# Windowed attention and a gated feed-forward on one core: a planner's order gives way to a table of 1334 numbers

## The chip, the cores and the metric

The kernel runs on 1 core of one Trainium2 chip. The metric is device time in microseconds (us) of one execution; less is better.

## The reference

Four batches of 768 tokens. Attention has 8 heads of 64; each chunk of 32 queries sees 8 memory keys and its own context of 56 keys (16 to the left, 8 to the right, fewer at the ends). Its output goes through a feed-forward network whose hidden layer is gated by a convolution over three tokens.

```python
for c in range(nc):                       # 24 chunks of 32 queries
    k_full = concat([mem_k, k[l_start:r_end]])
    scores = scale * q_c @ k_full.T
    a = exp(scores - max(scores))
    a = a / (sum(a) + 1e-9)
    out[c] = a @ v_full
x = out as (B, S, 512)
h = maximum(x @ w_in, 0.0)                # 512 -> 1024
conv_out = sum over k of conv_w[k] * h shifted by k - 1 tokens
return (h * sigmoid(conv_out)) @ w_out    # 1024 -> 512
```

All inputs but the weights are float32; the weights w_in, conv_w and w_out come as 64-bit floats and are turned into pairs of float32 numbers (hi and lo) on the chip.

## The kernel before, in words

Attention works in 32 steps, eight a batch: a step is one half of the tokens (hf) and two heads. The first four steps are groups of their own, the others go two by two, which makes 18 groups. A group loads q, k and v (L473), computes scores on the tensor engine (PE) into the psum tile s (L485), takes the maximum on the vector engine (DVE, L402), subtracts it (L408) and takes exp on the scalar engine (ACT, L414), or does both on ACT (L433). Sums (L451), 1e-9 (L455), reciprocal (L458) and the product that normalizes (L461) follow; 1e-9 and the product run on DVE or on GpSimd (POOL), by the strings ZADD and NORM. PE transposes the probabilities into tile t (L509), ACT copies them to w_t (L516), PE multiplies by v (L524), and ACT and DVE split the result into x_hi (L537) and x_lo (L540).

The feed-forward has eight blocks (fc) of 128 hidden features. For each block and half, PE adds up four times three products of x and w_in in one of four psum banks f (L563: hi by hi, hi by lo, lo by hi), and ACT takes the relu (L580). When both halves of a block are there, the convolution runs over all 768 tokens: the first tap on ACT (L590) or DVE (L594) by TAP, two more on DVE (L600); ACT takes the sigmoid (L604); the product with h is on DVE or POOL (L608) by MULT; ACT rounds to hi (L618) and DVE or POOL subtracts to get lo (L621) by LO. Then PE adds up eight times three products with w_out for each of six tiles of tokens, in a bank f again (L639), ACT copies it out (L651) and SP stores it (L654).

Sixteen blocks of weights, 512 KB each, are loaded (L285) into a ring of four tiles w64 and converted by from_f64: ACT takes the absolute value (L288), DVE shifts and masks (L292 to L339), POOL adds or multiplies (L334 to L357). W_IN and W_OUT name one of several ways for each.

What sets the order: every call of plan.op records an operation with its engine, a cost in ns, a due time, the tiles that it reads and writes. Plan.run then plays the whole program by these costs: an engine that is free takes, of the operations that could start at once, the one with the least due time (with a penalty for a change of the activation table or of PE's mode). The due times are linear in the step or block, with constants in DUE. Operations are emitted in the order in which this play started them, and each engine and queue works in the order of emission. All loads and stores are issued by SP into one queue. A tile comes from a ring with a fixed number of buffers: f has 4, w64 4, s and t one each; a new tile can be made only when the last use of the one that many places before has been emitted.

```python
            t, e, i = best
            ...
            do()
            self.times.append((t, end, e, i))
```

Of the kernel before, what the change touches and what calls it, by code (L numbers as in the profile page):

```python
# [2 lines left out]

# [5 lines left out]

# [6 lines left out]

CH, LEFT, RIGHT, NMEM = 32, 16, 8, 8  # L20
# [35 lines left out]
class Tile:


    def __init__(self, ring, make):
        self.ring, self.make, self.t, self.left, self.due = ring, make, None, 0, None  # L60


class Plan:

    def __init__(self):
        self.ops, self.last, self.readers = [], {}, defaultdict(list)
        self.rings, self.parts = {}, defaultdict(list)  # L70
# [4 lines left out]
    def op(self, eng, cost, due, do, r=(), w=(), shared=False, table=None, mode=None, late=70):  # L75

# [18 lines left out]
        tiles = dict.fromkeys(x[0] if isinstance(x, tuple) else x for x in (*r, *w))  # L95
        tiles = [x for x in tiles if isinstance(x, Tile)]
        for x in tiles:
            x.left += 1
# [4 lines left out]
    def over(self, k):

        if not isinstance(k, tuple):
            return [k, *self.parts[k]]
# [4 lines left out]
    def run(self):
        ops = self.ops
        n = len(ops)
        users = [[] for _ in range(n)]
        need = [0] * n
        for i, o in enumerate(ops):
            need[i] = len(o[4])
            for a in o[4]:
                users[a].append(i)
        ready = [0.0] * n  # L120
        cand = defaultdict(list)
        for i in range(n):
            if not need[i]:
                cand[ops[i][0]].append(i)
        free, shared_free, queue_free = defaultdict(float), 0.0, 950.0
        table = mode = None
        last_use = {}

        queue = defaultdict(list)
        for x in dict.fromkeys(x for o in ops for x in o[5]):  # L130
            queue[x.ring].append(x)
        for c in queue.values():
            c.sort(key=lambda x: x.due)
        self.times = []
        for _ in range(n):
            best = None
            for e, c in cand.items():
                at = []
                for i in c:
                    t = max(ready[i], free[e])  # L140
                    if ops[i][6]:
                        t = max(t, shared_free) if e == "V" else t
                    ok = True
                    for x in ops[i][5]:
                        if x.t is None:
                            size, used = self.rings[x.ring]
                            if queue[x.ring][len(used)] is not x:
                                ok = False
                                break
                            if len(used) >= size:  # L150
                                old = used[-size]
                                if old.left:
                                    ok = False
                                    break
                                t = max(t, last_use[old] + 70)
                    if ok:
                        at.append((t, i))
                if not at:
                    continue
                t0 = min(at)[0]  # L160
                i = min(
                    (ops[i][2] + (SWITCH if ops[i][7] and ops[i][7] != table else 0) + (MODE if ops[i][8] and ops[i][8] != mode else 0), i)
                    for t, i in at
                    if t <= t0 + 1
                )[1]
                if best is None or t0 < best[0]:
                    best = (t0, e, i)
            if best is None:
                raise RuntimeError("nothing can go on", [(i, *ops[i][:3], [x.ring for x in ops[i][5]]) for e in cand for i in cand[e] if e not in ('DMA','PE')][:12], dict((k, (len(v[1]), v[1][-v[0]].left if len(v[1])>=v[0] else 0, queue[k][len(v[1])].due if len(v[1])<len(queue[k]) else None)) for k, v in self.rings.items()))
            t, e, i = best  # L170
            eng, cost, due, do, after, tiles, shared, tab, md, late = ops[i]
            if tab and tab != table:
                cost += 1283
                table = tab
            if md and md != mode:
                cost += 95 if mode == "whole" else 140
                mode = md
            if e == "DMA":
                queue_free = max(queue_free, t + 600) + cost
                end, free[e] = queue_free + 1400, t + 60  # L180
            else:
                if shared:
                    t = max(t, shared_free)
                    shared_free = t + (cost * 0.78 if e == "G" else cost - 120)
                end = free[e] = t + cost
            cand[e].remove(i)
# [7 lines left out]
            self.times.append((t, end, e, i))
            for u in users[i]:
                ready[u] = max(ready[u], end + (late if ops[u][0] != e or e == "DMA" else 0))
                need[u] -= 1
                if not need[u]:
                    cand[ops[u][0]].append(u)
        return max(x[1] for x in self.times)  # L200


def vec(n, rate=1, ptr=0):
    return (140 + n / rate) / 0.96 + 62 * ptr


def act(n, psum=False, ptr=0):
    return ((192 if psum else 238) + n) / 1.2 + 93 * ptr

QB, KB, WB = 3, 2, 1

S_NS, A_NS = 520, 690
SWITCH, MODE = 78.9, 14.8


@with_exitstack  # L220
def attention_then_gated_ffn(
    ctx: ExitStack,
    tc: tile.TileContext,
    q: bass.AP,
    k: bass.AP,
    v: bass.AP,
    w_in: bass.AP,
    conv_w: bass.AP,
    w_out: bass.AP,
    out: bass.AP,  # L230
):
# [32 lines left out]

    def lin(name, i):
        return DUE[name][0] + DUE[name][1] * i

    def from_f64(src, hi, lo, key, n, kind, due, first):  # L270
# [535 lines left out]
```

## Time and profile before

| what | value |
|---|---|
| median of 3 runs | 359.49 us (358.17 to 363.31) |
| profiled execution, first to last instruction | 359.9 us |
| PE busy | 334.7 us |
| DVE, ACT, POOL busy | 244.8, 205.1, 126.4 us |
| mean granted clock of PE | 0.995 |
| read from memory, written | 35.55 MB, 6.29 MB |

The profile is of one execution. Its span runs from the first instruction to the last and is 0.4 us above the median of the runs, so little lies around it. Matmuls are pipelined: their records overlap, and a busy PE need not be at its peak. L485, L524 and L509 are float32; the trace has two matmuls and two weight loads where the program has one of L485 or L524.

### The profile page before, as it was taken

The numbers are of one execution on the slowest core, as the hardware profiler recorded it, in microseconds if no ns is written. First come the engines' busy times: TensorE is split into PE (matmuls) and PEld (weight loads), VectorE is DVE, ScalarE is ACT, GpSimd is POOL, SyncE is SP. The second block draws the span as 40 slices with busy tenths as digits, with TensorE's granted clock in tenths as the row PEclk, the third lists the DMA queues.
The fourth block names the chain that finished last, engine by engine and source line by source line (L and its number), as shares of the span: only waits on it lengthen the run. The fifth ranks groups of instructions, "written<-read, shape, count | busy, mean of one in ns | idle before, by whom it ended". The sixth has DMA issues, their size and how long they took to land.

```text
span 359.9 us, 10406 instructions
## 1 busy us (share of the span) xinstructions
PE 334.7 (93%) x4536; PEld 298.1 (83%) x4536; DVE 244.8 (68%) x319; ACT 205.1 (57%) x380; POOL 126.4 (35%) x154
## 2 busy tenths in 40 slices
PE   1497999996999999989999999999999999999996
PEld 0386999996999998778787889998887799998886
DVE  4877889997799899999993404889512228986100
ACT  3433666872978687779652417768453245584201
POOL 1566127922556636201656001252220001546000
PEclk9999999998999999999999999999999999999999
DMA  7978887777361153261202520000422000000111
GB/s 273 370 236 267 298 272 223 232 214 238 118 190 37 58 190 103 89 188 63 89 29 89 195 82 2 1 2 1 153 105 77 29 31 2 0 0 3 58 58 58
DMA packets 19917, 42.50 MB, mean 118 GB/s; under 512 B 2336, under 2 KB 10784, under 8 KB 19872
## 3 DMA queue, kind: packets, MB, share of 16 engines
q1 hardware_dynamic: 19872, 41.85, 35.1%
q8 instruction: 35, 0.57, 0.7%
q14 instruction: 10, 0.08, 0.1%
HBM read 35.55 MB, written 6.29 MB: 116 GB/s over the span
## 4 chain that ended last, share of the span: by engine, by line
PE 77%; DVE 13%; issue 4%; DMA 3%; ACT 2%; SPq 1%; POOL 0%; ACTq 0%; DVEq 0%
PE f L563 35%; PE f L639 27%; PE t L524 7%; PE s L485 4%; DVE c L600 4%; PE t L509 3%; DMA h<-in_k_dram 2%; DVE g L621 2%; DMA w<-in_w_out_dram 1%; DVE z L451 1%; SPq L473 1%; DVE x_lo L540 1%; DVE c L594 1%; DVE top L402 1%; DVE c L608 1%
## 5 line engine op out<-in xcount | busy, mean ns | idle before, releaser
L639 PE MATMUL f<-w_out_hi,g 128*128 128x512 f32 (+1 forms) x400 | 124.6, 388 | 0.1
L563 PE MATMUL f<-x_hi,w_in_hi 128*128 128x384 f32 x256 | 89.5, 349 | 0.0
L639 PEld LDWEIGHTS f<-w_out_hi,g 128*128 128x128 f32 x400 | 74.0, 188 | 16.5 <-DVE g L621 0.6
L563 PE MATMUL f<-x_hi,w_in_lo 128*128 128x384 f32 x256 | 86.9, 340 | 0.0
L563 PE MATMUL f<-x_lo,w_in_hi 128*128 128x384 f32 x256 | 86.8, 339 | 0.0
L639 PE MATMUL f<-w_out_lo,g 128*128 128x512 f32 (+1 forms) x200 | 77.1, 386 | 0.8 <-issue 0.8
L600 DVE SCALAR_TENSOR_TENSOR c<-h,cw,c 128x768 f32<-128x768 f32 x48 | 61.9, 1298 | 23.5 <-ACT c L590 22.1
L563 PEld LDWEIGHTS f<-x_hi,w_in_hi 128*128 128x128 f32 x256 | 48.6, 190 | 1.3 <-issue 0.5
L563 PEld LDWEIGHTS f<-x_hi,w_in_lo 128*128 128x128 f32 x256 | 48.8, 190 | 0.2
L563 PEld LDWEIGHTS f<-x_lo,w_in_hi 128*128 128x128 f32 x256 | 48.7, 190 | 0.0
L639 PEld LDWEIGHTS f<-w_out_lo,g 128*128 128x128 f32 x200 | 37.6, 188 | 8.8 <-issue 1.3
L608 POOL TENSOR_TENSOR c<-c,h 128x768 f32<-128x768 f32 x9 | 16.5, 1837 | 77.5 <-ACT c L604 75.4
L651 ACT COPY o_sb<-f 128x512 f32<-128x512 f32 (+1 forms) x25 | 14.2, 570 | 43.7 <-PE f L639 31.6
L580 ACT ACTIVATE h<-f 128x384 f32<-128x384 f32 x48 | 23.4, 491 | 21.6 <-PE f L563 21.1
L621 POOL TENSOR_TENSOR g<-c,g 128x768 fp32r<-128x768 f32 x12 | 25.7, 2144 | 22.0 <-ACT g L618 22.0
L604 ACT ACTIVATE c<-c 128x768 f32<-128x768 f32 x32 | 27.1, 846 | 10.4 <-DVE c L600 10.2
L524 PEld LDWEIGHTS t<-w_t,v_t 64*64 64x64 f32 x1536 | 25.4, 140 | 7.9 <-issue 4.3
L540 DVE TENSOR_TENSOR x_lo<-t,x_hi 128x768 fp32r<-128x768 f32 (+1 forms) x18 | 15.5, 862 | 23.5 <-ACT x_hi L537 23.4
L524 PE MATMUL t<-w_t,v_t 64*64 64x32 f32 x1536 | 27.5, 225 | 2.6 <-issue 1.3
L618 ACT CAST g<-c 128x768 fp32r<-128x768 f32 x24 | 20.0, 835 | 9.1 <-POOL c L608 6.4
L485 PE MATMUL s<-k_t,q_d 64*32 64x64 f32 x1344 | 18.6, 231 | 5.2 <-issue 4.7
L516 ACT COPY w_t<-t 128x768 f32<-128x768 f32 (+1 forms) x18 | 13.2, 732 | 17.4 <-PE t L509 17.4
(75 smaller groups left out, 439.0 us busy)
## 6 DMA issues: line engine op xcount, KB each, us to landing
v_t<-in_v_dram SPq DMA_DIRECT2D x32, 384.0 KB, 4.5
k_t<-in_k_dram SPq DMA_DIRECT2D x28, 252.0 KB, 4.1
out_dram<-o_sb SPq DMA_DIRECT2D x23, 256.0 KB, 2.0
q_d<-in_q_dram SPq DMA_DIRECT2D x28, 192.0 KB, 4.7
w<-in_w_in_dram SPq DMA_DIRECT2D x8, 512.0 KB, 5.2
w<-in_w_out_dram SPq DMA_DIRECT2D x8, 512.0 KB, 4.0
h<-in_k_dram SPq DMA_DIRECT2D x4, 252.0 KB, 7.0
h<-in_q_dram SPq DMA_DIRECT2D x4, 192.0 KB, 6.8
```

The source lines that it names most:

```text
L485: nc.tensor.matmul(s.t[w * CH : (w + 1) * CH, h ^ (w & 1), (i * NG + g) * KW : (i * NG + g + 1) * KW], lhsT=q_d.t[r, c], rhs=k_t.t[r, c * ...
L524: nc.tensor.matmul(t.t[h * D : (h + 1) * D, c & 1, c // 2 * CH : (c // 2 + 1) * CH], lhsT=vs[i].t[r, o], rhs=w_t.t[r, i, o], start=True, s ...
L540: lambda: nc.vector.tensor_tensor(out=lo(), in0=sums(), in1=hi().bitcast(F32), op=ALU.subtract),
L563: nc.tensor.matmul(f.t[:, :TW], lhsT=w_in_p[c][:, fc, cc], rhs=x_p[a].t[:, cc], start=(cc == 0 and i == 0), stop=(cc == NCC - 1 and i == 2),)
L580: nc.scalar.activation(h.t[:, 1 + o : 1 + o + TW], f.t[:, :TW], AF.Relu)
L600: lambda i=i: nc.vector.scalar_tensor_tensor(out=c.t, in0=h.t[:, i : i + S], scalar=w[i], in1=c.t, op0=ALU.mult, op1=ALU.add), (*H, c), (c ...
L604: plan.op("A", act(S), due, lambda: nc.scalar.activation(c.t, c.t, AF.Sigmoid), (c,), (c,), table="sigmoid")
L608: lambda: (nc.vector if mult == "V" else nc.gpsimd).tensor_tensor(out=y(), in0=c.t, in1=h.t[:, 1 : S + 1], op=ALU.mult), (c, h), (h if kee ...
L618: plan.op("A", act(S), due, lambda: nc.scalar.copy(out=g_hi(), in_=x()), (h,), (p[0],))
L621: lambda: (nc.vector if lo == "V" else nc.gpsimd).tensor_tensor(out=g_lo(), in0=x(), in1=g_hi().bitcast(F32), op=ALU.subtract), (h, p[0]), ...
L639: nc.tensor.matmul(ps.t[:, :n], lhsT=g[fc][a].t[:, tt * P : (tt + 1) * P], rhs=w_out_p[c][:, fc, o : o + n], start=(fc == 0 and i == 0), s ...
L651: plan.op("A", act(n, True), due[-1], lambda: nc.scalar.copy(out=o_sb.t[:, :n], in_=ps.t[:, :n]), (ps,), (o_sb,))
```

## The change

Plan.run no longer plays anything. A tuple ORDER holds the 1334 numbers of the recorded operations, each once, and run emits them in that order; it only asserts that what an operation needs has been emitted and that its tile's ring has room. Costs, due times and DUE go. The operations are the same, in the same numbering. Ring sizes, W_IN, W_OUT, SOFT and GROUP stay. Five strings that choose an engine change: TAP at 12 places of 32 (20 on ACT become 18), MULT at 17 (16 on POOL become 17), LO at 11 (16 on POOL become 9), NORM at 4 of 18 groups (10 on POOL become 8), ZADD at 12 (9 on POOL become 7). Lines of the new file are shorter, so the same operation has another line: L485 is L295, L524 L319, L540 L326, L563 L343, L600 L363, L608 L366, L621 L373, L639 L387, L285 L203, L314 L212, L473 L286.

```diff
-TAP = "AVVVAAVAAAVAVVAAAAAAVAAAAVVVVAAA"
-MULT = "VVVVVVGVVGGGGGVGGVGGVVVVVGGGVGGG"
-LO = "GGGGGVVVVVVVGGGGVVGGGVGVVVGGVVGV"
+TAP = 'AAAVAVAVAAVAVVAAAVVAAVAVAAVVVAVA'
+MULT = 'GGGGVVVVGVVGGGVGGGVGVVGVGVVVGVGG'
+LO = 'GVVGVVVVVVVVGVVGGVVVGVGVVVGVVGVV'
-NORM = "GGGGGGVVGGGGVVVGVVGGGVVVVVVGGGVG"
-ZADD = "GGGVGVVVVVGGVVVVVVGGGGGGVVVGGGVV"
+NORM = 'GGGGGGGVVGGGVVVGVVVGVVVVVVVGGGVG'
+ZADD = 'VVGGVVGVVVVGGVVVVVVGVGVGVVGGGGGV'
-DUE = {
-    "early": (-11.2, 1.02), "qk0": (-34.5, 3.94), "v0": (27.5, 7.26), "late": (-38.8, 4.05),
...
+ORDER = (
+    11, 12, 14, 79, 29, 28, 90, 45, 46, 63, 13, 15, 101, 80, 16, 17, 202, 206, 85, 86, 88, 81, 82, 83, 87, 84, 89, 62,
...
-    def run(self):
...
+    def run(self, order):
+        done = set()
+        assert sorted(order) == list(range(len(self.ops)))
+        for i in order:
+            do, after, tiles = self.ops[i]
+            assert after <= done, i
             for x in tiles:
                 if x.t is None:
+                    size, used = self.rings[x.ring]
+                    assert len(used) < size or not used[-size].left, i
                     x.t = x.make()
...
             do()
+            done.add(i)
```

PE, about 80 us into the profile before: the group t_1397 (L524) and the scores s_1481 (L485) in the order before. A row counts the program's matmuls, 48 of two rows standing for 96 in the trace.

```order
L563 MATMUL f_1411<-x_hi0_1371,w_in_hi_71 128x384
L563 MATMUL f_1411<-x_hi0_1371,w_in_lo_72 128x384
L563 MATMUL f_1411<-x_lo0_1382,w_in_hi_71 128x384
L524 MATMUL t_1397<-w_t_1415,v_t_882 64x32 x24
L524 MATMUL t_1397<-w_t_1415,v_t_1238 64x32 x24
L485 MATMUL s_1481<-k_t_1317,q_d_1141 32x64 x24
L485 MATMUL s_1481<-k_t_1328,q_d_1319 32x64 x24
L563 MATMUL f_1390<-x_hi1_737,w_in_hi_71 128x384
L563 MATMUL f_1390<-x_hi1_737,w_in_lo_72 128x384
L563 MATMUL f_1390<-x_lo1_776,w_in_hi_71 128x384
```

The two short kinds of matmul stand next to each other, with L563 on both sides.

PE, the same group (here t_1352, L319) in the new order:

```order
L343 MATMUL f_1368<-x_hi1_748,w_in_hi_71 128x384
L343 MATMUL f_1368<-x_hi1_748,w_in_lo_72 128x384
L343 MATMUL f_1368<-x_lo1_750,w_in_hi_71 128x384
L319 MATMUL t_1352<-w_t_1360,v_t_1249 64x32 x24
L319 MATMUL t_1352<-w_t_1360,v_t_1251 64x32 x24
L343 MATMUL f_1256<-x_hi1_748,w_in_hi_71 128x384
L343 MATMUL f_1256<-x_hi1_748,w_in_lo_72 128x384
L343 MATMUL f_1256<-x_lo1_750,w_in_hi_71 128x384
```

Behind it stand 15 matmuls of L343, these three among them, and then the scores s_1465 (L295):

```order
L343 MATMUL f_1331<-x_hi1_748,w_in_hi_71 128x384
L343 MATMUL f_1331<-x_hi1_748,w_in_lo_72 128x384
L343 MATMUL f_1331<-x_lo1_750,w_in_hi_71 128x384
L295 MATMUL s_1465<-k_t_1342,q_d_1344 32x64 x24
L295 MATMUL s_1465<-k_t_1340,q_d_1346 32x64 x24
L343 MATMUL f_1524<-x_hi0_1295,w_in_hi_71 128x384
```

The two short groups have moved apart.

SP, the start of the program, before (h are the tiles that hold q and k of the first four steps, w64 the raw weights):

```order
L285 DMA w64_78<-in_w_in_dram 128x1024
L473 DMA h_80<-in_q_dram 128x384
L473 DMA h_82<-in_k_dram 128x504
L473 DMA h_84<-in_q_dram 128x384
L473 DMA h_86<-in_k_dram 128x504
L285 DMA w64_88<-in_w_in_dram 128x1024
```

SP, the start of the program, now:

```order
L286 DMA h_78<-in_q_dram 128x384
L286 DMA h_80<-in_k_dram 128x504
L203 DMA w64_107<-in_w_in_dram 128x1024
L286 DMA h_109<-in_k_dram 128x504
L286 DMA h_111<-in_q_dram 128x384
L203 DMA w64_113<-in_w_in_dram 128x1024
```

The first weights have moved behind q and k of the first step.

DVE, about 90 us into the profile before: the last shift of L314 (of w64_1635, raw weights of w_out), and what stands behind it.

```order
L461 TENSOR_TENSOR e_1420<-e_1420,z_1564 128x768
L314 TENSOR_SCALAR w64_1635<-w64_1635 128x512
L319 SCALAR_TENSOR_TENSOR w64_1635<-w64_1635 128x512
L600 SCALAR_TENSOR_TENSOR c_980<-g_621,cw_75,c_980 128x768 x2
L445 MEMSET e_1643 32x2x2x16
L455 TENSOR_SCALAR z_1644<-z_1644 128x12
L458 RECIPROCAL z_1644<-z_1644 128x12
L540 TENSOR_TENSOR x_lo1_1726<-t_1553,x_hi1_1714 128x768
```

The last shift (of w64_1773, L212) in the new order, where x_lo1_1753 is the tile that x_lo1_1726 was:

```order
L206 TENSOR_SCALAR w_top_1873<-w_top_1873 128x512
L208 TENSOR_SCALAR w_top_1873<-w_top_1873 128x512
L209 SCALAR_TENSOR_TENSOR w_top_1873<-w64_1685,w_top_1873 128x512
L326 TENSOR_TENSOR x_lo1_1753<-t_1789,x_hi1_1719 128x768
L212 TENSOR_SCALAR w64_1773<-w64_1773 128x512
L214 TENSOR_SCALAR w64_1685<-w_top_1873 128x512
```

It has moved from ahead of the first x_lo of that tile to behind the second.

## Rows read from the trace of the kernel before

**Rows 1.** The page's head: span, and busy time of each engine.
```profile
span 359.9 us, 10406 instructions
PE 334.7 (93%) x4536; PEld 298.1 (83%) x4536; DVE 244.8 (68%) x319; ACT 205.1 (57%) x380; POOL 126.4 (35%) x154
```

**Rows 2.** Stretches: length; PE, weight loads, DVE, ACT, POOL busy; clock, DMA share, GB/s.
```profile
0.00:33.00 33.00, 18.45 (x599) 15.43 (x599) 23.46 (x53) 13.90 (x26) 14.12 (x22) 1.00 0.86 296
33.00:82.00 49.00, 46.23 (x1015) 43.37 (x1015) 43.90 (x75) 32.80 (x74) 24.77 (x34) 1.00 0.77 245
82.00:156.00 74.00, 71.45 (x1271) 64.90 (x1272) 65.81 (x84) 55.20 (x111) 35.52 (x39) 0.98 0.39 121
156.00:277.20 121.20, 119.51 (x1148) 103.07 (x1147) 75.66 (x75) 68.94 (x112) 34.40 (x43) 1.00 0.23 79
277.20:359.90 82.70, 79.02 (x503) 71.31 (x503) 35.99 (x35) 34.30 (x60) 17.56 (x17) 1.00 0.07 26
```

**Rows 3.** Waits of PE: who waited for whom, us in total, times, longest.
```profile
PE s L485 <- issue: 4.7, 2, 2.8
...
PE t L524 <- issue: 1.3, 1, 1.3
...
PE f L639 <- issue: 0.8, 1, 0.8
```

**Rows 4.** Timeline of PE: start, us, instruction, count, idle before and releaser.
```profile
34.64 0.31 PE L485 MATMUL s<-k_t,q_d 64*32 64x64 f32 x7 [1.94 <-issue]
...
78.76 1.60 PE L524 MATMUL t<-w_t,v_t 64*64 64x32 f32 x96
80.29 0.67 PE L485 MATMUL s<-k_t,q_d 64*32 64x64 f32 x42
83.76 0.96 PE L485 MATMUL s<-k_t,q_d 64*32 64x64 f32 x54 [2.80 <-issue]
...
157.14 0.89 PE L524 MATMUL t<-w_t,v_t 64*64 64x32 f32 x43 [1.27 <-issue]
```

**Rows 5.** The page's DMA queues: packets, MB, share of 16 engines' span.
```profile
q8 instruction: 35, 0.57, 0.7%
```

**Rows 6.** PE alone: two stretches (length, busy, clock, DMA), and two matmuls between.
```profile
84.00:86.00 2.00, 2.00 (x58) 0.56 0.51 138
...
212.30:245.60 33.30, 33.30 (x193) 1.00 0.03 9
...
85.46 0.52 PE L563 MATMUL f<-x_lo,w_in_hi 128*128 128x384 f32 x1
85.78 0.52 PE L563 MATMUL f<-x_hi,w_in_hi 128*128 128x384 f32 x1
```

**Rows 7.** The chain of waits from 140 to 180 us by line; timeline of DVE and POOL.
```profile
by line: DVE c L600 28.0%; DVE g L621 16.1%; issue 14.0%; DVE c L594 8.0%; DVE z L451 4.8%; DVE x_lo L540 4.6%; PE t L524 4.6%; PE s L485 2.9%; DVE e L461 2.5%; DVE top L402 2.2%; PE t L509 2.2%; DVE h L608 2.2%; DVE c L608 2.1%; ACT x_hi L
...
84.76 0.96 DVE L402 TENSOR_REDUCE top<-s 128x12 f32<-128x768 f32 x1 [0.76 <-PE s L485]
...
91.84 0.89 DVE L314 TENSOR_SCALAR w<-w 128x512 uint32<-128x512 uint32 x1 [3.26 <-DMA w<-in_w_out_dram]
...
171.18 2.30 DVE L621 TENSOR_TENSOR g<-h,g 128x768 fp32r<-128x768 f32 x1
...
170.76 1.91 POOL L608 TENSOR_TENSOR h<-c,h 128x768 f32<-128x768 f32 x1 [5.94 <-ACT c L604]
```

**Rows 8.** Timeline of the opening: the queue's issuer SP, PE and DVE.
```profile
1.62 0.42 SPq L473 DMA_DIRECT2D h<-in_k_dram  x1
...
5.86 0.96 PE L485 MATMUL s<-h 64*32 64x64 f32 x48 [5.86 <-DMA h<-in_k_dram]
...
18.93 0.56 DVE L540 TENSOR_TENSOR x_lo<-t,x_hi 128x384 fp32r<-128x384 f32 x1 [0.56 <-ACT x_hi L537]
```

**Rows 9.** Groups by shape: busy us, mean ns, idle before and releasers.
```profile
L621 DVE TENSOR_TENSOR g<-c,g 128x768 fp32r<-128x768 f32 x12 | 12.3, 1026 | 5.5 <-ACT g L618 5.5
...
L621 POOL TENSOR_TENSOR g<-c,g 128x768 fp32r<-128x768 f32 x12 | 25.7, 2144 | 22.0 <-ACT g L618 22.0
```

More of the change, by code (lines that the diff above doesn't have):

```diff
@@ L98, in op @@
             x.left += 1
-            x.due = due if x.due is None else x.due
-        self.ops.append((eng, cost, due, do, after - {i}, tiles, shared, table, mode, late))
-        return i
+        self.ops.append((do, after - {i}, tiles))
     def over(self, k):
@@ L109, in over @@
         return [k, k[0]]
-    def run(self):
[L112 to L186, printed above, removed]
@@ L191, in run @@
                 x.left -= 1
-                last_use[x] = max(last_use.get(x, 0), end + late)
             do()
[L194 to L204, printed above, removed]
@@ L207, in act, with attention_then_gated_ffn @@
[L207 to L217, printed above, removed]
-@with_exitstack
[L221 to L231, printed above, removed]
+            done.add(i)
+QB, KB, WB = (3, 2, 1)
+@with_exitstack
+def attention_then_gated_ffn(ctx: ExitStack, tc: tile.TileContext, q: bass.AP, k: bass.AP, v: bass.AP, w_in: bass.AP, conv_w: bass.AP, w_out: bass.AP, out: bass.AP):
@@ L265, in lin @@
[L265 to L288 removed]
+    w_in_p = [const.tile([P, NFC, NCC, P], F32R, name=f'w_in_{p}') for p in ('hi', 'lo')]
@@ new lines, in attention_then_gated_ffn, with from_f64, op @@
+    w_out_p = [const.tile([P, NFC, DM], F32R, name=f'w_out_{p}') for p in ('hi', 'lo')]
+    cw = const.tile([P, NFC * 3], F32, name='cw')
+    cw_p = [const.tile([P, NFC * 3], t, name=f'cw_{x}') for x, t in (('hi', F32R), ('lo', F32))]
+    def from_f64(src, hi, lo, key, n, kind):
+        w = tile_of('w64', W64, [P, WC, 2], U32)
+        x = tile_of('w_top', 2, [P, WC], U32)
+        low, up = (lambda: w.t[:, :n, 0], lambda: w.t[:, :n, 1])
+        top, ftop = (lambda: x.t[:, :n], lambda: x.t[:, :n].bitcast(F32))
+        flow, bits, fbits = (lambda: low().bitcast(F32), up, lambda: up().bitcast(F32))
+        L, U = ((w, 0), (w, 1))
+        V, A, G = (nc.vector, nc.scalar, nc.gpsimd)
+        def op(do, r, wr):
+            plan.op(do, r, wr)
+        plan.op(lambda: nc.sync.dma_start(out=w.t[:, :n].rearrange('p n w -> p (n w)'), in_=src.bitcast(U32)), w=(w,))
+        op(lambda: A.activation(ftop(), up().bitcast(F32), AF.Abs), (U,), (x,))
@@ L470, in load, with scores @@
             size *= x
-        plan.op(
-            "DMA", size * 4 / 400, due,
-            lambda: nc.sync.dma_start(out=tile.t.rearrange(flat) if flat else tile.t, in_=src), w=(tile,),
-        )
-    def scores(s, i, q_d, k_t, due):
+        plan.op(lambda: nc.sync.dma_start(out=tile.t.rearrange(flat) if flat else tile.t, in_=src), w=(tile,))
+    def scores(s, i, q_d, k_t):
         def mm():
@@ new lines, in ffn_in, with gate @@
+        plan.op(relu, (f,), ((h, hf),))
+    def gate(fc, h, tap, mult, keep=False):
+        c = tile_of('c', 3, [P, S])
+        w = [cw[:, 3 * fc + i:3 * fc + i + 1] for i in range(3)]
+        H = ((h, 0), (h, 1), 'cw')
+        if tap == 'A':
+            plan.op(lambda: nc.scalar.activation(c.t, h.t[:, 0:S], AF.Copy, scale=w[0]), H, (c,))
+        else:
+            plan.op(lambda: nc.vector.tensor_scalar(out=c.t, in0=h.t[:, 0:S], scalar1=w[0], scalar2=None, op0=ALU.mult), H, (c,))
+        for i in (1, 2):
+            plan.op(lambda i=i: nc.vector.scalar_tensor_tensor(out=c.t, in0=h.t[:, i:i + S], scalar=w[i], in1=c.t, op0=ALU.mult, op1=ALU.add), (*H, c), (c,))
+        plan.op(lambda: nc.scalar.activation(c.t, c.t, AF.Sigmoid), (c,), (c,))
+        y = (lambda: h.t[:, 1:S + 1]) if keep else lambda: c.t
+        plan.op(lambda: (nc.vector if mult == 'V' else nc.gpsimd).tensor_tensor(out=y(), in0=c.t, in1=h.t[:, 1:S + 1], op=ALU.mult), (c, h), (h if keep else c,))
+        return (h if keep else c, y)
@@ L625, in split, with ffn_out @@
+    def split(h, x, lo):
+        p = [tile_of('g', 2 * NFC, [P, S + 2], F32R) for _ in range(2)]
+        g_hi, g_lo = (lambda: p[0].t[:, :S], lambda: p[1].t[:, :S])
+        plan.op(lambda: nc.scalar.copy(out=g_hi(), in_=x()), (h,), (p[0],))
+        plan.op(lambda: (nc.vector if lo == 'V' else nc.gpsimd).tensor_tensor(out=g_lo(), in0=x(), in1=g_hi().bitcast(F32), op=ALU.subtract), (h, p[0]), (p[1],))
         return p
-    def ffn_out(b, g, tt, due, parts=1):
+    def ffn_out(b, g, tt, parts=1):
@@ L700, in attention_then_gated_ffn @@
     for fc in range(NFC):
-        convert("out", w_out[fc * P : (fc + 1) * P], w_out_p, fc, W_OUT[fc], lin("w_out", fc), lin("w_out_load", fc))
+        convert('out', w_out[fc * P:(fc + 1) * P], w_out_p, fc, W_OUT[fc])
     for tt in range(4):
-        ffn_out(0, g, tt, [lin("out0", fc) + 0.1 * tt for fc in range(NFC)])
+        ffn_out(0, g, tt)
     for tt in range(4, 6):
-        ffn_out(0, g, tt, [lin("out0b", fc) + 0.1 * tt for fc in range(NFC)])
-    y = [through_gate(1, fc, lin("gate1", fc), True) for fc in range(NFC)]
@@ L707, in attention_then_gated_ffn, with out_rest @@
-    g = [split(*y[fc], lin("split1", fc), LO[NFC + fc]) for fc in range(NFC)]
+        ffn_out(0, g, tt)
+    y = [through_gate(1, fc, True) for fc in range(NFC)]
+    g = [split(*y[fc], LO[NFC + fc]) for fc in range(NFC)]
     steps(16, 24)
-    t = DUE["out"][0]
-    def out_rest(b, g, t, last):
+    def out_rest(b, g, last):
         for tt in range(3):
-            ffn_out(b, g, tt, [t + 2.1 * fc + 0.1 * tt for fc in range(NFC)])
+            ffn_out(b, g, tt)
         for tt in range(3, 6):
-            ffn_out(b, g, tt, [t + 17 + 5.7 * (tt - 3) + 0.7 * fc for fc in range(NFC)], 2 if last and tt == 5 else 1)
@@ L730, in attention_then_gated_ffn @@
-    plan.run()
+        out_rest(b, g, b + 1 == B)
+    plan.run(ORDER)
 def _laid_out(q, k, v, mem_k, mem_v):
```

439 lines of the change are left out of this document (125 added, 314 removed), and 64 rows, old and new, of tables (DUE, ORDER).

## Prediction

> **What bounds the kernel now.** I read the page's head first, then stretches, then who waits for whom. The head shows TensorE (PE) busy for 334.7 of 359.9 us and VectorE (DVE) for 244.8 [rows 1]. So at most 25.2 us of PE's idle time can be had, and the question is where it lies. The table of five stretches tells it: PE is busy 18.45 of the first 33 us, 46.2 of the next 49, 71.5 of the next 74, and 119.5 of the 121.2 from 156.0 to 277.2 [rows 2]. Idle are thus 14.6 us in the opening, then 2.8, 2.5 and 1.7, and 3.7 in the last stretch, most of it the last eviction and the output's way to memory. Behind the opening PE is the bound, and it has few gaps.
>
> The list of waits names their cause: on PE's matmuls of L485, L524 and L639 it says "issue" for 4.7, 1.3 and 0.8 us, which means that nothing that the profile shows was waited for [rows 3]. The timeline shows the largest in the middle of a group: 42 of 96 score matmuls, a hole of 2.80 us, then the other 54; and likewise inside other groups, 1.94 us at 34.64 and 1.27 us at 157.14 [rows 4]. No operand is late in the middle of such a group. What these holes have in common is their distance. Between the hole at 34.64 and that at 83.76 lie 1015 matmuls and 1015 weight loads, 2030 instructions; then 2543, then 2296 [rows 2]. In units of 256 that is 7.9, 9.9 and 9.0. A DMA queue of kind "instruction" moved 35 packets and 0.57 MB [rows 5], 16.3 KB each; PE's 9072 listed instructions over 35 packets make 259 a packet, near enough to 256. I read the holes as PE waiting for its own next block of instructions. They come where PE runs through a block quickest: 96 matmuls of L524 stand directly ahead of 96 of L485, from 78.76 to 80.29 and on [rows 4], 384 instructions in about 2.7 us, while a block of L563 (0.17 us a matmul [rows 6]) lasts over 20 us.
>
> DVE is the second bound. The chain of waits for 140 to 180 us runs through its lines, 28% L600 and 16% L621, with 4.6% in L524 [rows 7]. PE still has work then, but DVE releases the last tiles of it.
>
> **The change part by part.** The same matmuls run; no work is removed.
>
> (a) PE's order behind the opening. Where scores s_1481 stood directly behind t_1397, 15 matmuls of L563 now stand between such groups (the listings of PE). I counted the new order in blocks of 256 from the same start, at 0.016, 0.012 and 0.17 us for matmuls of L524, L485 and L563 [rows 4, 6]. Behind the opening the shortest block lasts about 4.0 us; the old order has five of 1.8 to 3.0 us, and four of these held a hole. The new groups of L485 ahead of L524 (four of them late) don't get two block ends into one pair. So the three late holes go: 2.80 + 1.27 + 0.85 (the last within the 0.8 of L639) = 4.9 us. From both sides: none goes (0), or all do (4.9); below nothing if new short blocks formed, which the count excludes except for a late packet, up to 2.8 us. A short block and its hole made 3.0 to 4.9 us together (1.9 + 2.80 at 83.76), so new blocks of 4.0 to 4.6 us may keep some tenths each where transfers are dense. I take 4.9, and leave those tenths to the range.
>
> (b) The clock behind the hole. From 84 to 86 us the granted clock is 0.56 of full, which is its lower level of 1.2 GHz for most of it, after PE had stood still for 2.80 us; matmuls of L563 then start 0.32 us apart, where 193 of them took 33.30 us at the full clock, 0.17 each [rows 6]. From 84.65 to 87.76 PE did six such matmuls and six transposes: 3.11 us at the low level, about half of it at the high one. Without the hole this goes too: 1.5 us (bounds 0 and 1.6).
>
> (c) The opening. SP (the queue's issuer) now sends q and k of the first step ahead of the first weights, 444 KB instead of 956 KB to the end of k (the listings of SP). Before, k was issued at 1.62 and the first scores started at 5.86 [rows 8]. By sizes alone the scores come 1 to 1.5 us sooner and the weights about as much later. DVE takes the scores first now, and finishes step 0 ahead of step 1, where it had waited for step 1 first; its first x_lo came at 18.93 [rows 8]. Summing DVE's operations ahead of that x_lo by their own durations, I get 11 us instead of 12. But ahead of the fourth x_lo stand 27 us instead of 24.5, as more of the conversion of weights comes first. Against that the hole of 1.94 us at 34.64 should go, as the pair of L524 and L485 there is turned round. Bounds: 4 us gained (sooner scores, no hole) to 2 us lost (weights late). I take 1.9, the hole alone.
>
> (d) Operations on other engines. LO moves seven subtractions of L621 from POOL to DVE, MULT one product back, two norms and two taps come to DVE. One L621 takes 1.03 us on DVE and 2.14 on POOL [rows 9]. Through batches 0 and 1, where DVE bounds, the count is five L621 more, two products and one tap fewer on DVE: about 5.2 - 2.2 - 0.9 = 2 us more work. In return POOL holds DVE up less: beside one POOL product of 1.91 us an L621 took 2.30 [rows 7] instead of 1.03, so 1.3 us were lost. POOL loses some 7 us of such work there (five times 2.14 less two products), worth 0 to 4.7 us to DVE at that rate. Net on DVE between 2 lost and 2.7 gained; I take 0.5 gained, near the middle since POOL often works beside a DVE that needs nothing of it.
>
> (e) DVE's own stalls, which must go for (a) to pay. DVE stood 3.26 us until 91.84 for a transfer of w_out, with two L600 and the next x_lo queued behind it [rows 7]. That operation stood ahead of the first x_lo1; its counterpart now stands behind the second (the listings of DVE), while its transfer has only two rows more ahead of it on SP. I take this wait as gone; what is late next is the w_out block itself, which PE needs only from the first L639. With 1.9 from the opening, 3.3 here, 0.8 that DVE lost behind the late scores (it waited until 84.76 [rows 7]) and 0.5 from (d), DVE comes forward by 6.5 us; PE by 1.9 + 2.8 + 1.5 + 1.3 = 7.5. The two agree to a microsecond, so little of PE's gain is given back there. If the cover fails, the waits return on PE one to one.
>
> Waits that the table adds: I moves between L563 and L639, three matmuls of each in turn, tie PE to ACT's evictions of four f banks; queued behind a late one is all of PE. Before, 192 matmuls of L563 ran in a row without a hole. I price this at nothing, since behind 190 us DVE and ACT are busy less than two thirds of the time [rows 2], and keep up to 2.8 us for the range.
>
> Sum: 4.9 + 1.5 + 1.9 = 8.3 us off the profiled span of 359.9, so 351.6 us. The span is 0.4 us above the median of the runs shown, 359.49; I make no correction for that. A change of less than 2%, 7.2 us, can't be told from none by a measurement like this one.
>
> The Trainium skill, "Runtime: NRT & Kernel Launch", section "Instruction fetch mechanics", says that instructions come in 16 KiB blocks of 256 and that crossing a block's end is mostly hidden, so that order would not matter to it. The holes at equal distances speak against the word "hidden" here [rows 2, 4], while the block's size agrees; by the page's rule (a) and (b) would give nothing and the sum would be 358.0.
>
> **Rivals.** First, a better one: the opening gains its full 4 us and DVE's relief reaches 2.7; PE then has no hole and starts sooner: 359.9 - 4.9 - 1.5 - 4 = 349.5, or less. For it: DVE's first x_lo has less ahead of it. Against: the fourth has more.
>
> Second, DVE stays the bound. The w_out wait only moves, POOL's relief is nothing and the 2 us of added work remain. Then of PE's 8.3 us only the opening's 1.9, the last hole's 0.85 and the 0.8 behind the scores hold, less 2: 358.4. For it: the chain of rows 7. Against: the wait has one named cause, and the new order puts other work in front.
>
> Third, the holes are not a matter of order, or a late packet makes new ones: (a) and (b) give nothing and 358.0 remains. For it: block ends without a hole exist, so chance has a share. Against: the distances.
>
> Fourth, slower. DVE takes ten more operations net, and each meets POOL as the L621 of rows 7 did, 2.30 us instead of 1.03. If these lie on the chain, 10 x 2.3 = 23 us come on and, with 8.3 off, 374 would result; from 16 us on, about seven such operations, it is over 2% slower (367). Against: DVE is idle for 115 us in all.
>
> **How the numbers follow.** Forecast, 350 to 353.5: 0.45. The better one, 346 to 350: 0.22. DVE bound: 0.15. Holes remain: 0.12. Slower: 0.06. The line at 2% is 352.3; two thirds or a little more of the forecast's own range lie below it, 0.32, and with the better one faster has 0.54. Same gets 0.13 + 0.15 + 0.12 = 0.40, slower 0.06. The range from 346.0 to 358.0 leaves out the slower case and the far ends.
>
> **What would show it.** Right: no "issue" wait over 1 us on PE behind 40 us, a granted clock of 1.00 from 40 us on, PE's busy time unchanged near 333 us and its idle time down to 17; a DVE without the 3 us wait for w_out. Wrong: waits of PE on DVE's L373 or L326 between 120 and 190 us that add up to more than 2 us; holes of PE inside groups; a first x_lo later than 19 us; PE idle behind 190 us for ACT.

## The result, and the profile after

The changed kernel takes 355.91 us (median of 6 executions, 355.01 to 358.46), the kernel before 359.95 (6 executions, 358.17 to 363.31). The ratio is 0.9886, 95% interval 0.9839 to 0.9932: 4.0 us are gained, where 8.3 were forecast. That is below 2%; the direction was right, the size a little under half.

An execution's time lies some 2 us above its span: the profiled one after took 356.13 us with a span of 354.1. The profiled execution of before, with its span of 359.9 [rows 1], therefore stands near 361.9 by estimate, some 2 us above its kernel's median, and not 0.4 as it looked when its span was set against times. The two traces differ by 5.8 us, the medians by 4.0. The experiments below ran in four rounds, in which the kernel before had medians of 360.3 to 360.95; their ratios are to the kernel before of the same round, and small differences between rounds are read from the ratios.

The page's head after, and the five stretches (columns as in [rows 1, 2]):

```profile
span 354.1 us, 10383 instructions
PE 333.4 (94%) x4536; PEld 296.3 (84%) x4536; DVE 244.9 (69%) x331; ACT 201.1 (57%) x378; POOL 111.0 (31%) x144
```
```profile
0.00:33.00 33.00, 19.76 (x613) 16.49 (x613) 24.89 (x58) 13.54 (x24) 14.32 (x20) 1.00 0.83 290
33.00:82.00 49.00, 46.88 (x1063) 43.45 (x1064) 45.08 (x76) 33.91 (x75) 23.16 (x35) 1.00 0.69 232
82.00:156.00 74.00, 72.45 (x1176) 64.81 (x1175) 71.20 (x91) 56.38 (x114) 33.17 (x36) 1.00 0.39 124
156.00:277.20 121.20, 120.64 (x1211) 104.93 (x1210) 71.03 (x78) 66.38 (x118) 28.63 (x41) 1.00 0.26 84
277.20:354.10 76.90, 73.70 (x478) 66.58 (x477) 32.70 (x31) 30.89 (x48) 11.76 (x14) 0.99 0.08 28
```

Against [rows 2], PE is busy 1.3 us more in the first stretch and idle only 0.56 us in the fourth (1.69 before); the clock is full from 33 to 277 us. But from 82 to 156 us DVE is now busy 71.2 of 74 us (65.8 before). The waits of PE behind 30 us:

```profile
PE t L310 <- DVE x_lo L326: 1.4, 2, 0.9
PE s L295 <- issue: 1.2, 2, 0.9
PE t L310 <- DVE e L279: 1.0, 1, 1.0
PE f L387 <- DVE g L373: 0.6, 1, 0.6
```

No "issue" wait over 1 us is left where [rows 3] showed 2.8 and 1.3. In their place stand 3.0 us of waits for DVE. (Lines of after: scores L295, transposes L310, values L319, input product L343, output product L387, x_lo L326, norm L279, product L366, g_lo L373; in the kernels of the experiments the same code stands a few lines higher.)

Where the gain went shows if each matmul is counted at the rate of an undisturbed group (0.0122 us for scores, 0.016 values, 0.095 transposes, 0.1735 and 0.233 for the two products; 325.5 us in all, in both) and that sum is taken off the moment at which PE got there. PE's loss so far, in us, at the first matmul that starts at or behind each moment:

| at us | 33 | 42 | 70 | 90 | 100 | 116 | 160 | 345 |
|---|---|---|---|---|---|---|---|---|
| before | 22.7 | 23.3 | 24.6 | 29.8 | 29.9 | 30.7 | 34.1 | 36.5 |
| after | 20.0 | 21.5 | 24.1 | 25.1 | 25.8 | 28.3 | 28.8 | 30.4 |
| ahead by | 2.7 | 1.8 | 0.5 | 4.7 | 4.1 | 2.4 | 5.3 | 6.1 |

The column at 33 already holds the hole of before that ends at 34.64: at 32 us the losses are 20.6 and 19.8, a lead of 0.8 us, and the other 1.9 of the 2.7 come with that hole. 2.2 of the 2.7 are gone by 70. The holes and the low clock of before return 4.2 by 90, and 2.3 of the lead go again between 90 and 116; 2.9 come by 160 and 0.8 behind it. So the gains add up to 10.6 us, and 4.5 are given back.

### The profile page after: what moved, and what is told of

It reads as the page before. It is cut to its first block, busy times and chain, and to the rows that moved or that the text cites. A ratio compares the mean times of both kernels' runs of the same rounds, so it can differ in the third digit from the quotient of the medians.

```text
span 354.1 us, 10383 instructions
## 1 busy us (share of the span) xinstructions
PE 333.4 (94%) x4536; PEld 296.3 (84%) x4536; DVE 244.9 (69%) x331; ACT 201.1 (57%) x378; POOL 111.0 (31%) x144
## 4 chain that ended last, share of the span: by engine, by line
PE 64%; DVE 18%; issue 7%; ACT 4%; POOL 3%; DMA 2%; SPq 0%; DVEq 0%; POOLq 0%; ACTq 0%
PE f L387 32%; PE f L343 22%; PE t L319 5%; PE s L295 3%; PE t L310 2%; DVE c L363 2%; POOL c L366 2%; DVE w_top L209 2%; DVE x_lo L326 2%; DVE e L279 2%; DMA w<-in_w_in_dram 2%; DVE top L253 1%; DVE g L373 1%; DVE w L213 1%; DVE z L276 1%
## 5 line engine op out<-in xcount | busy, mean ns | idle before, releaser
L387 PE MATMUL f<-w_out_hi,g 128*128 128x512 f32 (+1 forms) x400 | 127.6, 388 | 0.6 <-DVE g L373 0.6
L343 PE MATMUL f<-x_hi,w_in_hi 128*128 128x384 f32 x256 | 89.6, 350 | 0.0
L387 PEld LDWEIGHTS f<-w_out_hi,g 128*128 128x128 f32 x400 | 73.9, 188 | 16.1 <-DVE g L373 1.2
L343 PE MATMUL f<-x_hi,w_in_lo 128*128 128x384 f32 x256 | 86.6, 338 | 0.0
L343 PE MATMUL f<-x_lo,w_in_hi 128*128 128x384 f32 x256 | 86.5, 338 | 0.0
L387 PE MATMUL f<-w_out_lo,g 128*128 128x512 f32 (+1 forms) x200 | 77.0, 385 | 0.0
L363 DVE SCALAR_TENSOR_TENSOR c<-h,cw,c 128x768 f32<-128x768 f32 x48 | 55.9, 1180 | 13.4 <-ACT c L359 12.4
L343 PEld LDWEIGHTS f<-x_hi,w_in_hi 128*128 128x128 f32 x256 | 48.5, 189 | 2.3 <-issue 0.2
L343 PEld LDWEIGHTS f<-x_hi,w_in_lo 128*128 128x128 f32 x256 | 48.5, 189 | 1.1
L343 PEld LDWEIGHTS f<-x_lo,w_in_hi 128*128 128x128 f32 x256 | 48.4, 189 | 0.0
L366 POOL TENSOR_TENSOR c<-c,h 128x768 f32<-128x768 f32 x8 | 14.0, 1746 | 96.7 <-ACT c L364 96.6
L387 PEld LDWEIGHTS f<-w_out_lo,g 128*128 128x128 f32 x200 | 37.6, 188 | 6.6
L326 DVE TENSOR_TENSOR x_lo<-t,x_hi 128x768 fp32r<-128x768 f32 (+1 forms) x18 | 15.5, 860 | 22.0 <-ACT x_hi L325 22.0
L319 PEld LDWEIGHTS t<-w_t,v_t 64*64 64x64 f32 x1536 | 25.2, 140 | 4.2 <-issue 2.0
L319 PE MATMUL t<-w_t,v_t 64*64 64x32 f32 x1536 | 27.2, 224 | 0.1
L361 DVE TENSOR_SCALAR c<-h,cw 128x768 f32<-128x768 f32 x11 | 8.0, 727 | 27.4 <-ACT h L351 27.2
L269 ACT ACTIVATE e<-s,top 128x64 f32<-128x64 f32 x88 | 20.1, 337 | 1.6 <-DVE top L258 1.2
L373 DVE TENSOR_TENSOR g<-c,g 128x768 fp32r<-128x768 f32 x17 | 18.3, 1084 | 3.8 <-ACT g L372 3.8
```

The source lines that it names most:

```text
L269: nc.scalar.activation(e.t[r, g, i, c], s_()[r, i, g, c], AF.Exp, bias=top.t[r, g, i:i + 1], scale=SCALE, accum_out=z.t[r, g, i:i + 1] if ...
L319: nc.tensor.matmul(t.t[h * D:(h + 1) * D, c & 1, c // 2 * CH:(c // 2 + 1) * CH], lhsT=vs[i].t[r, o], rhs=w_t.t[r, i, o], start=True, stop= ...
L326: plan.op(lambda: nc.vector.tensor_tensor(out=lo(), in0=sums(), in1=hi().bitcast(F32), op=ALU.subtract), (t, *keys(x_hi)), keys(x_lo))
L343: nc.tensor.matmul(f.t[:, :TW], lhsT=w_in_p[c][:, fc, cc], rhs=x_p[a].t[:, cc], start=cc == 0 and i == 0, stop=cc == NCC - 1 and i == 2)
L363: plan.op(lambda i=i: nc.vector.scalar_tensor_tensor(out=c.t, in0=h.t[:, i:i + S], scalar=w[i], in1=c.t, op0=ALU.mult, op1=ALU.add), (*H, ...
L366: plan.op(lambda: (nc.vector if mult == 'V' else nc.gpsimd).tensor_tensor(out=y(), in0=c.t, in1=h.t[:, 1:S + 1], op=ALU.mult), (c, h), (h ...
```

## The experiments

**Are the holes set by the count of instructions?** Both kernels, with PE's block ends moved.

```diff
+    pad = bank('f', 4)
+    def fill():
+        for _ in range(22):
+            nc.tensor.matmul(pad.t[:CH, :KW], lhsT=ident[:D, :CH], rhs=ident[:D, :KW], start=True, stop=True)
+    plan.op(fill, (), (pad,))
     plan.run(ORDER)
```

The changed kernel with it. 

> The changed kernel with 88 more PE instructions (22 small matmuls, 0.5 us, into an unused bank) in the idle time behind the first scores, so that every block of 256 instructions ends 88 earlier. By the count five blocks of 1.8 to 1.9 us then appear, ending near 41, 110, 165, 182 and 250 us. Theory (holes come from block ends that PE reaches too soon): three to five new holes of 0.8 to 2.8 us inside groups there, 360 to 366 us. Rival (a hole's place is not set by the count, the new order is what removed them): no new hole, 355.5 to 357.

Measured: 367.99 us, ratio to before 1.0218 (1.0138 to 1.0297), about 12 us more than without and above the 360 to 366 expected. The timeline of PE shows five holes of over 1 us, each inside a group, and the windows behind them the clock (length, busy, clock, DMA share, GB/s):

```profile
42.94 0.43 PE L290 MATMUL s<-k_t,q_d 64*32 64x64 f32 x26 [1.36 <-issue]
...
120.83 0.66 PE L314 MATMUL t<-w_t,v_t 64*64 64x32 f32 x29 [1.45 <-issue]
...
178.99 0.42 PE L314 MATMUL t<-w_t,v_t 64*64 64x32 f32 x11 [1.29 <-issue]
...
198.83 0.53 PE L314 MATMUL t<-w_t,v_t 64*64 64x32 f32 x18 [1.52 <-issue]
...
268.45 0.43 PE L314 MATMUL t<-w_t,v_t 64*64 64x32 f32 x16 [1.09 <-issue]
...
42.90:46.00 3.10, 3.06 (x36) 0.61 0.94 312
121.00:124.50 3.50, 3.50 (x40) 0.65 0.96 280
179.00:182.00 3.00, 3.00 (x23) 1.00 0.90 260
198.90:203.20 4.30, 4.30 (x30) 0.69 0.08 27
268.50:272.00 3.50, 3.50 (x39) 1.00 0.61 219
```

They are the five counted ones; the later four come 11 to 18 us later than said, because the count was turned into time with the opening's loss alone. Matched matmul by matmul, this run ends 10.3 us behind the changed kernel.

The kernel before with it (its order written as a table). 

> The kernel before with the same 88 PE instructions put behind its first scores; nothing else differs. By the count the short blocks that ended at the holes of 34.64, 83.76 and 157.14 us are gone; three others appear, ending near 39, 255 and 273 us. Theory: no hole at 84 and 157 us, no low clock behind 84, and new holes of 0 to 2 us near 255 and 273: 355.5 to 359 us. Rival (place not set by the count): holes at 84 and 157 stay, 359.5 to 361.

Measured: 366.8 us, 1.019 (1.0151 to 1.0228): the places came as counted, the time did not. The holes at 34.64, 83.76 and 157.14 are gone; new ones stand here:

```profile
44.35 0.46 PE L290 MATMUL s<-k_t,q_d 64*32 64x64 f32 x14 [3.42 <-issue]
...
260.69 0.51 PE L290 MATMUL s<-k_t,q_d 64*32 64x64 f32 x34 [1.32 <-issue]
...
280.51 0.66 PE L290 MATMUL s<-k_t,q_d 64*32 64x64 f32 x40 [1.53 <-issue]
```

The first is longer than any of before, and behind it the granted clock is 0.50 from 44.40 to 49.80 us. Which block ends where is settled by these two runs; how long a hole gets was not foreseen. The trace's packets of the instruction queue show what the holes end with. In the kernel before one packet runs from 81.33 to 82.21 us:

```profile
q8 instruction: 1, 0.02, 5.5%
```

(queue, packets, MB and share from 81.3 to 82.3 us), none follows it ahead of 84.8, and PE resumes at 83.76. Others end at 33.13 and 155.77 and PE resumes at 34.64 and 157.14, so 1.4 to 1.6 us behind the packet each time; in the run above it is 42.89 and 44.35.

**Order against engines.** The five strings that name engines, and the table, exchanged singly.

```diff
-NORM = 'GGGGGGGVVGGGVVVGVVVGVVVVVVVGGGVG'
+NORM = 'GGGGGGVVGGGGVVVGVVGGGVVVVVVGGGVG'
...
```

All five as before, in the new order. 

> The new order, but each tap, product, norm, subtraction and small sum on the engine it had before. Theory: the gain is in PE's order (block ends) and the opening, and the engine moves are worth less than 1.5 us either way: 354.5 to 357.5 us, three late holes absent. Rival: the moved work is what the new order needs to keep PE's operands in time; without it the waits of PE on DVE between 33 and 115 us grow from about 3.6 to over 6 us: 359 us or more.

Measured: 371.19 us, 1.0319 (1.0257 to 1.0382). The rival was right that the moved work is needed, and its time came true, but not the waits that it named: PE waited for DVE only 1.2 us between 33 and 115 us (2.4 after). The losses came later, on a norm of POOL at 118.30 (3.4 us), on subtractions at 145, 178 and 343 us (1.0, 1.1 and 2.8) and by the low clock behind the first and the last. POOL's timeline shows the dearest place:

```profile
114.83 1.28 POOL L221 TENSOR_TENSOR w_top<-w_top,w 128x512 f32<-128x512 f32 x1
116.07 2.18 POOL L279 TENSOR_TENSOR e<-e,z 128x768 f32<-128x768 f32 x1
```
```profile
118.30:126.50 8.20, 8.20 (x206) 0.50 0.51 150
```

One norm, on POOL behind a sum, held PE's transposes until 118.30 (114.68 after), and the clock then was at its lower level for 8.2 us: about 6 us together by matching matmuls in this execution (PE was 1.3 us behind ahead of the wait, 7.5 after the slow stretch).

The old order with the new engines. 

> The old order of operations, written as a table, with the new engines. Theory: PE's stream is the old one, so the holes near 34, 84, 157 and 277 us and the low clock behind 84 us stay: 358.5 to 361.5 us. Rival: the engine moves carry the gain: 357 or less.

Measured: 364.39 us, 1.0137 (1.0087 to 1.0186). The holes stay, shorter (1.73 us at 83.92, 0.77 at 158.18), and the new engines alone cost 4 us, which neither expectation had. So each half of the change loses, 10.9 and 4.1 us, and both together gain 4.0.

The strings in three parts, new order. 

> The changed kernel with only the eleven subtractions g_lo (L373) whose engine changed put back. Theory: the order alone is not the matter; each moved operation matters where a DVE or POOL queue is about to release PE. Two waits of PE on g_lo appeared with all engines put back (1.3 and 1.4 us, near 143 and 177 us), so 357.5 to 360. Rival: subtractions are hidden, 355.5 to 357.

> The changed kernel with only the norms (L279) and small sums (L277) put back, four and twelve of them. Theory: one norm of 2.2 us on POOL, queued behind POOL's 1.3 us sum of a weight, holds PE's transposes near 115 us for 3 to 4 us, and the clock falls behind it: 359 to 364. Rival: one norm is absorbed by other slack: 355.5 to 357.

> The changed kernel with only the products (L366) and taps (L359, L361) put back, 17 and 12 of them. Theory: the first four products go back to DVE, 0.95 us each, where it has no idle time between 84 and 116 us, and the last batch's operands come late near 330 us (3 us and a low clock with all engines put back): 358 to 363. Rival: less of POOL beside DVE makes up for it: 354 to 357.

Measured: 358.16 (0.9921, 0.9891 to 0.9951), 359.09 (0.9942, 0.9913 to 0.9972) and 365.71 us (1.0138, 1.008 to 1.0196). Against the kernel before of their round, 360.9, these are 2.7 and 1.8 less and 4.8 more, where the changed kernel had 4.0 less. So putting back costs 1.3, 2.2 and 8.9 us, 12.4 together, where all five at once cost 14.9. Only the third is clear of the noise; the intervals of the first two overlap that of the changed kernel. The times lie inside the theory's range twice, by little for the norms, and above it for the products and taps. The waits near 143 and 177 that the first theory named did not come back; PE waits 1.62 us for the norm at 114.78 there (1.04 after). In the second PE's transposes waited 2.57 us for POOL's norm, until 116.10, and the clock was low behind that in the profiled execution (360.59 us), the third slowest of ten. In the third PE waits 2.42 us for one g_lo at 264.27, and the granted clock is 0.50 from 117 to 122 us and 0.64 from 264.3 to 269.

**POOL beside DVE.** A part of POOL's work is left out.

```diff
-        plan.op(lambda: (nc.vector if mult == 'V' else nc.gpsimd).tensor_tensor(...
+        plan.op(lambda: None if quiet else (nc.vector if mult == 'V' else nc.gpsimd).tensor_tensor(...
...
+    return gate(fc, hs[b, fc][0], TAP[i], MULT[i], keep, i < 4)
```

> The changed kernel with POOL's four products of batch 0 left out (no tensor is multiplied there; 7.5 us of POOL's work, three of them between 84 and 116 us). DVE keeps all its instructions. Theory (POOL beside DVE makes DVE slow, and that is what makes x_lo and the norm late for PE at 103 and 114 us): the norm that took 2.04 us and the bit operation that took 1.83 beside these products fall to 0.95 and 0.42 or near, DVE comes 2 to 3 us sooner, the two waits of PE shrink from 2.2 us to under 1: 353 to 355. Rival (DVE simply has too many instructions there): durations and waits stay, 355.5 to 357.

DVE of the changed kernel, and POOL beside it (start, us):

```profile
95.24 1.48 DVE L363 SCALAR_TENSOR_TENSOR c<-g,cw,c 128x768 f32<-128x768 f32 x1
...
98.78 2.04 DVE L279 TENSOR_TENSOR e<-e,z 128x768 f32<-128x768 f32 x1
100.75 0.41 DVE L206 TENSOR_SCALAR w_top<-w_top 128x512 f32<-128x512 f32 x1
101.19 0.43 DVE L208 TENSOR_SCALAR w_top<-w_top 128x512 uint32<-128x512 uint32 x1
101.66 1.66 DVE L209 SCALAR_TENSOR_TENSOR w_top<-w,w_top 128x512 uint32<-128x512 uint32 x1
103.24 0.94 DVE L326 TENSOR_TENSOR x_lo<-t,x_hi 128x768 fp32r<-128x768 f32 x1
...
105.22 1.83 DVE L214 TENSOR_SCALAR w<-w_top 128x512 uint32<-128x512 uint32 x1
```
```profile
97.68 2.32 POOL L366 TENSOR_TENSOR c<-c,g 128x768 f32<-128x768 f32 x1 [1.71 <-ACT c L364]
...
104.97 1.72 POOL L366 TENSOR_TENSOR c<-c,g 128x768 f32<-128x768 f32 x1
```

and DVE's same instructions without the products:

```profile
94.22 1.00 DVE L363 SCALAR_TENSOR_TENSOR c<-g,cw,c 128x768 f32<-128x768 f32 x1
...
97.28 0.96 DVE L279 TENSOR_TENSOR e<-e,z 128x768 f32<-128x768 f32 x1
...
99.07 0.69 DVE L209 SCALAR_TENSOR_TENSOR w_top<-w,w_top 128x512 uint32<-128x512 uint32 x1
...
101.95 2.13 DVE L214 TENSOR_SCALAR w<-w_top 128x512 uint32<-128x512 uint32 x1
```

Measured: 354.24 us, 0.9827 (0.9762 to 0.9892), 1.7 us less, with intervals that overlap. The norm fell from 2.04 to 0.96 us, L209 from 1.66 to 0.69, and the x_lo of 103.24 ends 3.5 us sooner: POOL's products had made them slow. L214 stayed slow (2.13), beside a subtraction of POOL (101.70 to 103.73) that came forward into its time, so only 1.8 us are left at the next x_lo. The wait at 103 is gone, that at 113 stays at 0.9. Matched by matmuls PE ends 1.7 us sooner, but 1.0 of that is there at 52 us, ahead of any product (no wait for instructions at 50, where the changed kernel had 0.86); 0.7 us is the products'. That POOL's products slow DVE is shown by these rows. What it costs PE is read from one execution of each: 0.7 us, and DVE came 1.8 sooner at the second x_lo where 2 to 3 were expected.

**DVE's order.** First three moves, then two others:

```diff
-... 130, 9, 291, 221, 222, ... 570, 571, 572, ... 407, ... 739, ... 461, ... 755, ... 724, 740, ...
+... 130, 291, 221, 222, 9, ... 407, 570, 571, 572, ... 739, 740, ... 461, ... 755, ... 724, ...   (three moves)
+... 130, 9, 291, 221, 222, ... 407, 570, 571, 572, ... 739, ... 724, 740, 461, ... 755, ...       (tile first)
```

> The changed kernel with three operations of DVE moved in the table, no engine changed: the x_lo of 41.91 us ahead of the last conversion of conv_w, the x_lo of 103.24 ahead of three conversions of w_out, the norm of 113.58 directly behind its reciprocal (ahead of a subtraction, a softmax subtraction and an x_lo). Theory (DVE bounds PE there, and what counts is what stands ahead of the tile that PE waits for): PE's three waits, 1.2, 0.7 and 1.3 us beyond the steady rate, vanish; 352.5 to 354.5 us. Rival (DVE's total work is the matter; PE then waits for the next tile): 355 to 357.

Measured: 360.32 us, 0.9966 (0.9931 to 1.0001): above both ranges and above the changed kernel, with intervals that just touch. The first move did bring PE forward by 1.0 us at 42 us and the second removed the wait near 104, but PE then stood longer for instructions: 1.34, 0.59 and 0.68 us at 50, 64 and 69 us, where the changed kernel had 0.86 and 0.34. The third put the x_lo last, and the x_lo holds the one t tile that the transposes write: a wait of 3.0 us at 116.68, with a clock of 0.68 behind it.

> The changed kernel with DVE's order altered at two places only: the x_lo of 103.24 us ahead of three conversions of w_out, and near 111 us the x_lo and the norm, both of which the next transposes need (the x_lo reads the one t tile that they write), ahead of a subtraction g_lo and a softmax subtraction. Theory (what stands ahead of PE's tile on DVE decides, and the run with three moves failed because it put the x_lo last): transposes at 113.3 instead of 114.68, the waits of 0.7 and 1.3 us gone, no new one: 353.5 to 355 us. Rival (whatever is put back is late next, or POOL's work lands on the new order): 355.5 to 357.5.

Measured: 358.24 us, 0.9932 (0.9899 to 0.9966), above both ranges; the interval overlaps that of the changed kernel, so no gain is shown, and no loss. The rival's mechanism fits, as PE still waits at 95.47, 115.00 and 116.65 (0.69, 1.16 and 0.80 us). DVE's rows show what happened to the conversions:

```profile
102.42 1.50 DVE L201 TENSOR_SCALAR w_top<-w_top 128x512 f32<-128x512 f32 x1
103.95 1.95 DVE L203 TENSOR_SCALAR w_top<-w_top 128x512 uint32<-128x512 uint32 x1
105.94 1.92 DVE L204 SCALAR_TENSOR_TENSOR w_top<-w,w_top 128x512 uint32<-128x512 uint32 x1
...
108.56 2.23 DVE L215 SCALAR_TENSOR_TENSOR w<-w 128x512 f32<-128x512 uint32 x1
```

The first three are the conversions of 0.41, 0.43 and 1.66 us above (L206, L208, L209; the last is 0.69 without the products), moved to later and now beside POOL's four operations from 102.36 to 110.2. In both orders some operation of DVE is slowed there; that this holds for every order is not shown.

**The opening.** The first load of w_in before or behind q and k, in each order.

```diff
-    11, 12, 14, 79, 29, 28, 90,
+    79, 11, 12, 14, 29, 28, 90,
```

> The changed kernel with the first load of w_in put back ahead of q and k on SP. Theory (the opening's gain is the earlier first scores): first scores back near 5.9 us, first x_lo from 16.9 to 18.5 or later, 357 to 359 us. Rival (conversion of the weights is what binds by 30 us): 355 to 356.5.

> The kernel before with q and k of the first step ahead of the first load of w_in on SP, nothing else. Theory: first scores near 4 us, but DVE still takes step 1 ahead of finishing step 0, so the first x_lo gains less than 1.5 us; the holes stay: 358.5 to 360.5 us. Rival (SP's order alone makes the opening's 3 us): 357 or less.

Measured: 357.29 us (0.9902, 0.9872 to 0.9933) and 362.44 us (1.0048, 1.0017 to 1.008). In the first, the scores start at 6.22 instead of 3.96, the first x_lo at 18.03 instead of 16.95, and PE ends 2.0 us later; the medians differ by 1.4, within their intervals. The time is the theory's; the x_lo comes a little sooner than its 18.5. In the second the scores start at 3.92, but DVE still begins with the conversion of the weights, which now land later (7.82 instead of 4.35), and takes the first maximum at 10.41; the second scores start at 11.66 instead of 9.18 and the first x_lo at 21.40 instead of 18.93. Neither expectation foresaw a loss. The new order of SP did not pay with DVE's old one.

## Why the prediction was half right

- **(a) and (b), the late holes and the clock: right.** None of the three returns and the clock is full where it was 0.56. Of 4.9 us, 1.2 stayed as new small waits at 50.88 and 69.18, the "some tenths" kept for the range. The two shifted kernels show the reason as it was given. The Trainium skill, "Runtime: NRT & Kernel Launch", section "Instruction fetch mechanics", calls the crossing of a block's end mostly hidden; here it cost up to 3.4 us.
- **(c), the opening: the hole as taken, and 0.8 us more.** 2.7 us at 33 us against 1.9. The hole that ended at 34.64 is 1.9 of them; the other 0.8 is what is left at 32 us of the scores' earlier start (3.96 instead of 5.86), with two new waits for instructions on the way (1.07 us at 17.04, 1.26 at 18.95). With the first weights put back ahead of q and k, PE is 2.0 us later at 32 us.
- **(d) failed.** "I take 0.5 gained" priced the moves by busy time. With the order fixed, putting them back costs 14.9 us, most of it by the products and taps. A move's price is where its operation stands: one norm, about 6 us in one execution.
- **(e) failed, and is the step that cost the forecast its size**: "so little of PE's gain is given back there". It took DVE's coming forward, 6.5 us, as enough for PE's 7.5. The w_out wait did go, but by the x_lo of 112.7, whose counterpart stood at 117.4, DVE had come forward by 4.6 us only. Before and after, up to that x_lo:

```profile
0.00:117.36 117.36, 98.28 (x2201) 90.89 (x2202) 97.05 (x173) 72.37 (x163) 57.75 (x85) 0.99 0.70 228
0.00:112.72 112.72, 96.85 (x2285) 87.99 (x2286) 100.35 (x169) 72.55 (x160) 58.89 (x82) 1.00 0.73 246
```

DVE is idle 7.9 us less (20.3, then 12.4) but busy 3.3 us more, in 169 instructions instead of 173, where (d) had counted 0.5 us less. PE gave back 2.2 us between 33 and 70 us and 2.3 between 90 and 116, earlier than the 120 to 190 named. Of the second, 0.7 us is POOL's products beside DVE, by the run without them. Of the first, 0.9 is the wait for the x_lo at 42.99 and 1.2 the waits for instructions. PE's idle time fell to 20.7 us, not to the 17 named. The waits for instructions depend on when PE arrives, but not on that alone: the run with three moves came sooner and waited longer (1.34 us), but the run with the old products and taps came at 49.30, sooner than the changed kernel's 49.70, and did not wait; its packet had ended at 47.77, against 49.59. What sets the packet's time stays open, and how the rest divides too.
- **The base**: "I make no correction for that" set a span against times. Taken as time, 359.9 is about 361.9; some 2 us of the missing 4.3 were never in the kernel's median.

## What to carry to other kernels

Before moving work between engines, look at what it stands in front of, and beside; an order and its engines that were tuned together did not come apart here. Where an engine runs many short instructions, count its instruction blocks: 22 matmuls in the wrong place cost more than the whole change gains. Set spans against spans.

## What the runs showed of the hardware

Some operations of DVE suffer beside POOL and others never. In the changed kernel the norm L279 (both inputs in SBUF) takes a median of 0.95 us alone and 1.69 beside POOL's longer ones, a 0.42 us bit operation up to 1.83, g_lo up to 2.53; the reductions L253 and L276 and the subtractions from PSUM L255 and L326 (128x768 at most) never took over 0.96. The Trainium skill, "SBUF — State Buffer", section "Who interferes with whom", says that DVE shares one pair of ports with GpSimd (POOL), that two SBUF inputs or a two-port mode contend, and that a reduction never does; the trace agrees for the norm and the reductions, and does not show in which mode the bit operation ran.

A short stop can cost the clock as well: in the changed kernel with 88 more PE instructions it was 0.61 to 0.69 behind the holes of 1.36, 1.45 and 1.52 us, and full behind those of 1.29 and 1.09. The length alone does not decide it: the clock stayed full behind 1.94 us at 34.64 in the kernel before and 1.53 at 280.51 in the old order with the 88 instructions.

In the opening the clock column's 1.00 does not fit the rows. In the changed kernel matmuls of L343 start 0.32 us apart at 24.80 and 25.12, as at the lower level in [rows 6], and 0.18 apart at 25.66 and 25.84; in the kernel before the same change comes between 25.88 and 26.73. By these rows both openings ran at the lower level until about 26 us.
